# Norm stores and inverse-block loads moved to GpSimd's queue, keys loaded a step later: a chunked RWKV-7 with a SoLU block

## The chip, the cores and the metric

The kernel runs on one core of one Trainium2 chip. The metric is the device time of one execution in microseconds (us). Before the change it was 652.03 us, the median of three runs (650.71, 652.03 and 653.35).

A core has five engines that run at the same time, each with its own list of instructions that it works off in order: TensorE (PE in the profile; PEld are its weight loads), VectorE (DVE), ScalarE (ACT), GpSimd (POOL) and SyncE (SP). They wait for one another through semaphores. SP does no arithmetic here, it only issues DMA transfers; ACT and POOL issue some as well, each from its own list.

## What is computed

Two blocks in a row. The first is a recurrence over 768 tokens, for 4 batches of 8 heads of width 40; its outputs are rows of 320 numbers for 3072 tokens. The second is a feed-forward block with the SoLU activation and a layer norm.

```python
for t in range(S):                                   # S = 768, D = 40, state is D x D per head
    y[:, :, t] = einsum('bhd,bhde->bhe', rt, state)
    Sa = einsum('bhde,bhe->bhd', state, at)
    state_decay = state * wt[:, :, None, :] - einsum('bhd,bhe->bhde', Sa, bt)
    state = state_decay + einsum('bhd,bhe->bhde', vt, kt)
...
h = x @ w_in                                         # x: 3072 x 320, w_in: 320 x 1024
sm = softmax(h)
solu = h * sm
ln = (solu - mean) / sqrt(var + 1e-6) * g_ln
out = ln @ w_out                                     # w_out: 1024 x 320
```

## The kernel before

**Steps.** The recurrence is cut into chunks of 64 tokens. A step i works on one chunk of one pair of batches, with all 8 heads: 12 chunks times 2 pairs make N = 24 steps. Inside a chunk the recurrence becomes matrix products, and one triangular matrix of 64 x 64 for each head must be inverted. That matrix, nt, is made by `norm(i)`: TensorE multiplies a and b (both scaled by the decay), VectorE masks the product (L351), and the result is stored in HBM (`nt_dram`).

**Inverses.** Two steps share one inverse n = i // 2. `invert(n)` first calls `spread(n)`, which loads the 32 x 32 diagonal blocks of both steps' matrices back from HBM in another layout, with four transfers to the tile `blk`. The stored matrices must have landed first. Then VectorE copies and negates half of the blocks (L397) and runs 30 substitution steps of one product (L403) and one subtraction (L405) each. The result goes to HBM (`uu_dram`, L410), and `bring(i)` loads it for each step, into the tiles tu and uh, when it has landed. `flip(i)` transposes part of tu on VectorE (L430). `invert` is a Python generator: `some(n)` takes n substitution steps of it, so that they are spread between other work of VectorE.

**The loop.** The main loop (L774) runs i from -1 to 27 and works on several steps at a time. For step i it finishes the recurrence (`carried`, `driven`, `solved`, `answered`, `read`, `leave`). For i+1 it makes the score matrices (`attend_kv`, `attend_rs`, `scores`, `couple`, `close`). For j = i+5 it prepares the decayed a and b (`front`, which turns a with TensorE, L323, and multiplies it on VectorE, L347) and `norm(j)`, and after every second norm begins an inverse. For steps before i it computes the feed-forward block (`hidden`, `exped`, `weighed`, `spreadof`, `folded`, `output`).

**Order.** The lists of PE, POOL, DVE and SP follow the order of the program's text; only ACT's is arranged by a scheduler. So a transfer leaves SP when all that the program issues on SP before it has been issued and its own waits are met. In a step, SP's list is: `bring(i+1)` (tu and uh), `load_values(i+2)` (v), the keys, the store of `norm(j)`, in every second step the four loads of `spread`, the store of a finished inverse (wherever `some` comes to its end), and four transfers xT of `leave(i)`. POOL's list is: r of `load_values`, b and k scaled by the decay (`scaled(j+1)`, L318, tile kb), six transfers xT of `left(i-1)`, the power rs of the layer norm (L669), two copies v and r (`by_value(i+2)`, L296), and two multiplications of the state st (`leave`, L611).

**Keys.** `load_keys(i, names)` loads w, b, a and k of step i, in two transfers of 80 KB each (L265). w, b and k have three buffers each, a has four.

**Weights.** The feed-forward weights come as 64-bit floats in two words. `land` loads a part of them, and `narrow` and `split` turn the part into 32-bit numbers on VectorE and ScalarE (L182 to L195), between substitution steps, up to i = 3. When a part is done, POOL issues the load of a later one into the freed buffer (L208, L171). `centre_w2` (L218) needs all of w_out.

**Before the loop.** Steps 0 to 3 get their norms, inverse 0 is run and inverse 1 begun. The text from L758 on ends with the last substitution steps of inverse 0, its two `bring` calls, and the keys of steps 5 to 7.

Of the kernel before, what the change touches and what calls it, by code (L numbers as in the profile page):

```python
# [21 lines left out]
GRP = 2  # L22
# [26 lines left out]
def kernel(  # L49
# [18 lines left out]
    nc = tc.nc  # L68
# [67 lines left out]
    def banks(name):  # L136
        return ps1.tile([P, 2, 512], FP32, tag="banks", name=name)
# [12 lines left out]
    def land(n, queue):  # L150
        if n >= len(lands) + NF:
            return
        flat = w2.rearrange("p c n -> p (c n)")
        if n < len(lands):
            kt, x = lands[n]
            if n in (2, 3):
                to = two.tile([P, 512], I64, tag=("e", "lnT")[n - 2], name="bits", bufs=1)
            else:
                y = (0, 1, None, None, 0)[n]
                to = flat[:, 1024 * y:1024 * y + 1024].bitcast(I64)  # L160
            y = 0
            for at in (x,) if kt < 2 else (0, 1):
                for first, last in IN_ROWS[kt]:
                    queue.dma_start(out=to[y:y + last - first], in_=moe_w_in[first:last, 512 * at:512 * at + 512])
                    y += last - first
            landed[n] = [(w_in[:, 2 * kt + x], to, None)]
        else:
            c = n - len(lands)
            tag = ("bits", "e", "lnT", "bits", "e", "lnT", "bits", "lnT")[c]
            to = two.tile([P, DM if tag == "bits" else 512], I64, tag=tag, name="bits", bufs=1)[:, 0:DM]  # L170
            queue.dma_start(out=to, in_=moe_w_out[c * P:(c + 1) * P, :])  # L171
            landed[n] = [(w2[:, c], to, c)]
# [53 lines left out]
    def half(p):  # L226
        return slice(C * p, C * p + C)
# [6 lines left out]
    def in_turn(tile_of, some=units):  # L234

        lots = {}
        for u in some:
            lots.setdefault(tile_of(*u), []).append(u)
        lots = list(lots.values())
        return [lot[n] for n in range(max(map(len, lots))) for lot in lots if n < len(lot)]  # L240

    def mm(o, lhsT, rhs, start=True, stop=True):
        nc.tensor.matmul(o, lhsT=lhsT, rhs=rhs, start=start, stop=stop, skip_group_check=True)  # L243
# [13 lines left out]
    blocks, inverse = {}, {}  # L257
# [4 lines left out]
    def load(x, ap, i, queue=nc.sync):  # L262
        bp, ci = where_(i)
        for p in range(2):
            queue.dma_start(out=x[half(p), :, 0:D],  # L265
                              in_=ap[2 * bp + p, :, ci * C:(ci + 1) * C, :].rearrange("h t d -> t h d"))

    def ok(i):
        return 0 <= i < N


    def load_keys(i, names, queue=nc.sync):
        if not ok(i):
            return
        for n, ap in (("w", w), ("b", b), ("a", a), ("k", k)):
            if n in names:
                x = a_t[i % 4] if n == "a" else two.tile([P, H, D], FP32, tag="raw_" + n, name="raw_" + n,
                                                             bufs=3)
                st[i]["raw_" + n] = x
                load(x, ap, i, queue)  # L280

    def load_values(i):
        if not ok(i):
            return
        d = st[i]
        d["lv"] = two.tile([P, H, W2], FP32, tag="lv", name="lv", bufs=3)
        d["raw_r"] = two.tile([P, H, D], FP32, tag="raw_r", name="raw_r")
        load(d["lv"][:, :, C:], v, i)
        load(d["raw_r"], r, i, nc.gpsimd)
# [37 lines left out]
    def tokens(name, bufs=1):  # L327
        return two.tile([P, 2, 4, C], FP32, tag=name, name=name, bufs=bufs)
# [12 lines left out]
    def front(i):  # L341
        if not ok(i):
            return
        d = st[i]
        t = turned("a", d["raw_a"])
        aT = d["aT"] = tokens("aT", AHEAD)
        nc.vector.tensor_tensor(out=aT[0:W2], in0=t, in1=d["ex"][0:W2, :, :, 0:C], op=ALU.mult)  # L347
        d["bT"] = kept("bT", turned("b", d["kb"][:, H:]))

    def masked(dst, t):  # L350
        nc.vector.tensor_tensor(out=dst, in0=t.rearrange("p b (j c) -> p b j c", j=4),  # L351
                                in1=tri.unsqueeze(1).unsqueeze(1).to_broadcast([P, 2, 4, C]), op=ALU.mult)

    def keyed(t, u):
        p, q, g, h = u
        return t[rows(h), p, 2 * q + g]
# [5 lines left out]
    def norm(i):  # L362
        if not ok(i):
            return
        d = st[i]
        t = banks("pnt")
        for u in in_turn(lambda p, q, g, h: (h, p ^ h)):
            p, q, g, h = u
            j = 2 * q + g
            mm(t[half(p ^ h), h, j * C:j * C + C], keyed(d["bT"], u), keyed(d["aT"], u))  # L370
        nt = d["nt"] = tokens("nt", AHEAD)
        masked(nt, t[:, :, 0:256])
        n, at = divmod(i, GRP)
        if at == 0:
            blocks[n] = dram.tile([2 * GRP * H, C, C], FP32, tag="nt_dram", name="nt_dram")
        nc.sync.dma_start(out=blocks[n].rearrange("(a h x) s c -> a x s h c", a=GRP, x=2)[at].rearrange("x s h c -> (x s) h c"),
                          in_=nt.rearrange("p h j c -> p (h j) c"))


# [1 line left out]
    def spread(n):  # L381
        nb = two.tile([P, Q, Q], FP32, tag="blk", name="blk")
        for y in range(2):
            for e in range(2):
                home = C * y + Q * e
                queue = nc.gpsimd if y and not n else nc.sync
                queue.dma_start(out=nb[home:home + Q], in_=blocks[n][:, Q * e:Q * e + Q, Q * e:Q * e + Q])
        return nb

# [24 lines left out]
    def bring(i):  # L414
        if not ok(i):
            return
        d = st[i]
        d["tu"], d["uh"] = tu_t[i % 2], uh_t[i % 2]
        n, at = divmod(i, GRP)
        src = inverse[n].rearrange("(e a h x) c t -> e a h x c t", e=2, a=GRP, x=2)  # L420
        for x in range(2):
            nc.sync.dma_start(out=d["tu"][C * x:C * x + Q, :, Q:2 * Q], in_=src[0, at, :, x].rearrange("h c t -> c h t"))
        for x in range(2):
            nc.sync.dma_start(out=d["uh"][C * x + Q:C * x + C], in_=src[1, at].rearrange("h x c t -> c (h x) t"))

    def flip(i):
        if not ok(i):
            return
        tu = st[i]["tu"]
        nc.vector.transpose(out=tu[:, :, 0:Q], in_=tu[:, :, Q:2 * Q])  # L430
# [270 lines left out]
    def some(n):  # L701
        while steps and n:
            if next(steps[0], steps) is steps:
                steps.pop(0)
            else:
                n -= 1
# [52 lines left out]
    load_keys(6, "w")  # L759
    land(3, nc.sync)  # L760
    some(14)
    bring(0)
    bring(1)
    load_keys(7, "w")
    load_values(1)
    load_keys(5, "bak")
    for n in (4, len(lands)):
        land(n, nc.sync)
    load_keys(6, "bak")


    shares = {-1: (0, 6, 2, 6), 0: (0, 6, 4, 6), 1: (0, 6, 3, 6), 2: (0, 6, 3, 6), 3: (0, 6, 3, 6)}
# [1 line left out]
    for i in range(-1, N + 3 + LAG):  # L774
        j, m = i + AHEAD, i - LAG
        pieces = shares.get(i, (3, 6, 0, 6))
        some_weights = narrowed.get(i, (0, 0))

        some(pieces[0])
        if i >= 1:  # L780
            bring(i + 1)
        if i >= 0:
            load_values(i + 2)
        carried(i)
        driven(i)
        front(j)
        hidden(m - 2, ((0, 1),))
        load_keys(j + 4, "w")
        load_keys(j + 3, "bak")
        narrow(some_weights[0], pieces[1])  # L790

        solved(i)
        attend_kv(i + 1)
        hidden(m - 2, ((1, 1),))
        attend_rs(i + 1)
        hidden(m - 2, ((2, 0), (2, 1)))
        exped(m - 2)
        decay_turned(j + 1)
        scaled(j + 1)
        left(i - 1)  # L800

        answered(i)
        norm(j)
        if i >= 0:
            flip(i + 1)
        weighed(m - 2)
        spreadof(m - 2)
        decay(j + 2)
        if i == 0:
            turn_g()  # L810
        if i == 3 + LAG:
            centre_w2()
        output(m - 3, 0)
        if ok(j) and j % GRP == GRP - 1:
            begin_inverse(j // GRP)
        some(pieces[2])
        scores(i + 1)
        if i < 0:
            flip(i + 1)
        couple(i + 1)  # L820
        output(m - 3, 1)
        narrow(some_weights[1], pieces[3])

        close(i + 1)
        read(i, True)
        read(i, False)
        by_value(i + 2)
        leave(i)
        folded(m - 2)
        hidden(m - 1, ((0, 0), (1, 0)))  # L830
# [30 lines left out]
```

## Time and profile before

| | |
|---|---|
| median of three runs | 652.03 us |
| the profiled execution's own time | 652.45 us |
| its span, first to last instruction | 650.4 us |
| mean granted TensorE clock | 0.922 |
| TensorE busy (PE) | 562.9 us, 87% |
| TensorE weight loads (PEld) | 400.0 us, 61% |
| VectorE busy | 483.2 us, 74% |
| ScalarE busy | 245.0 us, 38% |
| GpSimd busy | 221.2 us, 34% |
| SP's DMA queue, share of 16 DMA engines | 40.8% |
| POOL's DMA queue, share of 16 DMA engines | 5.9% |

The shares are means over a program with stages that differ. The page's second part cuts the span into 40 slices of 16.3 us and gives the busy tenths of each engine: TensorE stands at 9 from about 195 us to the end, and between 2 and 8 ahead of that; VectorE stands at 7 to 9 from about 33 to 553 us, except for the slices of 65 to 81, 98 to 114 and 179 to 195 us, which show a 6, a 3 and a 6.

A time in the trace is counted from the span's start. `SPq` marks the issue of a transfer by SP. It isn't the transfer: the time shown there is the one in which SP was held by it. On POOL too the row `DMA_DIRECT2D` is the issue. What the data took afterwards is seen where somebody waits for it, or in the chain of waits.

### The profile page before, as it was taken

Reading aid. Unit: us, or ns where it says so; the run is one execution under the profiler, and the core shown is the slowest. Engines: PE = TensorE matmul, PEld = TensorE weight load, DVE = VectorE, ACT = ScalarE, POOL = GpSimd, SP = SyncE. Lnnn points to the kernel's source line nnn. Section 1 sums busy time; section 2 is a strip of 40 time slices with the busy share of each in tenths; the row PEclk is TensorE's granted clock in tenths of the full one; section 3 lists DMA queues with packets and bytes.
Section 4 is the critical chain, followed back from the end, with each engine's and each line's share of the span. In section 5 each row is a group of like instructions: output and inputs, shape, how many; then the busy total and the mean of one; then the engine's idle time right before and its main releaser. Section 6 shows DMA issues by size and latency. Waiting matters only on the chain.

```text
span 650.4 us, 26703 instructions
## 1 busy us (share of the span) xinstructions
PE 562.9 (87%) x11449; PEld 400.0 (61%) x11449; DVE 483.2 (74%) x1285; ACT 245.0 (38%) x497; POOL 221.2 (34%) x384
## 2 busy tenths in 40 slices
PE   5245474887889999999999999999999999999994
PEld 3134462765657676767677667767676767666653
DVE  4678693989967878979888889889897787333431
ACT  3413343355333344244434433443344324332221
POOL 3333222545414234514441453245233422322200
PEclk9666577589799999999999999999999999999998
DMA  8939796667363465466465555554432612310000
GB/s 164 160 70 151 126 164 118 145 128 135 63 106 64 88 113 102 95 112 115 81 114 92 109 96 99 96 100 94 78 70 58 109 38 48 62 38 25 23 20 20
DMA packets 276748, 59.92 MB, mean 92 GB/s; under 512 B 264656, under 2 KB 274488, under 8 KB 276632
## 3 DMA queue, kind: packets, MB, share of 16 engines
q1 hardware_dynamic: 263384, 44.96, 40.8%
q0 software_dynamic: 7856, 8.76, 5.9%
q10 hardware_dynamic: 5392, 4.51, 2.4%
q8 instruction: 90, 1.47, 1.0%
q14 instruction: 26, 0.21, 0.1%
HBM read 40.10 MB, written 13.37 MB: 82 GB/s over the span
## 4 chain that ended last, share of the span: by engine, by line
PE 67%; DVE 15%; DMA 10%; issue 3%; SPq 3%; ACT 1%; POOL 0%; DVEq 0%; POOLq 0%; ACTq 0%
PE h L243 15%; PE po L691 15%; PE pyo L243 7%; DVE prod L403 4%; DVE uu L405 4%; PE px L243 4%; PE pu L243 3%; PE plnT L680 3%; PE ps L243 3%; DMA blk<-nt_dram 3%; DMA nt_dram<-nt 2%; PE pl L243 2%; SPq L265 2%; PE pz L243 2%; PE pk L323 2%
## 5 line engine op out<-in xcount | busy, mean ns | idle before, releaser
L243 PE MATMUL h<-w_in,xT 128*128 128x512 f32 (+1 forms) x288 | 121.0, 612 | 0.0
L403 DVE TENSOR_TENSOR prod<-blk,uu 128x30 f32<-128x30 f32 (+4 forms) x360 | 107.9, 300 | 12.4 <-DMA blk<-nt_dram 2.4
L691 PE MATMUL po<-w,lnT 128*128 128x320 f32 x384 | 113.6, 441 | 3.0 <-DVE w L222 3.0
L405 DVE TENSOR_TENSOR uu<-uu,prod 128x30 f32<-128x30 f32 (+4 forms) x360 | 103.8, 288 | 12.4
L691 PEld LDWEIGHTS po<-w,lnT 128*128 128x128 f32 x384 | 70.4, 190 | 32.6 <-issue 5.8
L669 POOL TENSOR_TENSOR rs<-c,mhalf 128x1 f32<-128x1 f32 x24 | 13.4, 560 | 210.4 <-DVE c L668 210.4
L643 DVE TENSOR_REDUCE nmax<-h 128x1 f32<-128x1024 f32 x24 | 29.4, 1224 | 57.2 <-PE h L243 57.2
L611 POOL TENSOR_TENSOR st<-tot,ex 104x160 f32<-104x160 f32 x44 | 21.3, 501 | 102.4 <-DVE tot L607 102.4
L243 PEld LDWEIGHTS h<-w_in,xT 128*128 128x128 f32 (+1 forms) x288 | 38.8, 189 | 21.4 <-issue 19.3
L623 POOL DMA_DIRECT2D xT<-x x96 | 48.9, 515 | 0.0
L243 PE MATMUL pyo<-lv,kb 64*64 64x104 f32 x768 | 38.3, 272 | 4.9 <-DVE lv L351 2.3
L681 ACT COPY lnT<-plnT 128x512 f32<-128x512 f32 x48 | 26.1, 589 | 43.3 <-PE plnT L680 39.5
L646 ACT ACTIVATE e<-h,nmax 128x1024 f32<-128x1024 f32 x24 | 26.7, 1114 | 28.7 <-DVE nmax L643 27.6
L442 ACT ACTIVATE wy<-py,cst 128x256 f32<-128x256 f32 x24 | 11.4, 474 | 69.3 <-PE py L243 69.3
L243 PE MATMUL pyo<-lu,kb 64*64 64x104 f32 x768 | 37.0, 265 | 0.0
L265 POOL DMA_DIRECT2D raw_r<-in_r_dram x48 | 34.5, 720 | 0.1
L652 DVE TENSOR_TENSOR e<-h,e 128x1024 f32<-128x1024 f32 x24 | 28.8, 1199 | 5.8 <-ACT e L646 5.8
L592 DVE TENSOR_TENSOR x<-pyo,ex 104x256 f32<-104x256 f32 x48 | 18.1, 420 | 18.9 <-PE pyo L243 18.1
L318 POOL TENSOR_TENSOR kb<-raw_b,inv 128x320 f32<-128x320 f32 x24 | 21.4, 891 | 30.5 <-DMA raw_b<-in_b_dram 21.0
L660 DVE BATCH_NORM_STATS2 bs<-e 128x6 f32<-128x512 f32 x48 | 30.9, 685 | 0.8
L695 ACT ACTIVATE osb<-po,rs 128x320 f32<-128x320 f32 x24 | 12.7, 528 | 48.5 <-PE po L691 27.7
L243 PEld LDWEIGHTS pyo<-lv,kb 64*64 64x64 f32 x768 | 23.6, 143 | 10.3 <-issue 7.7
(124 smaller groups left out, 1110.6 us busy)
## 6 DMA issues: line engine op xcount, KB each, us to landing
nt_dram<-nt SPq DMA_DIRECT2D x24, 256.0 KB
blk<-nt_dram SPq DMA_DIRECT2D x46, 128.0 KB
raw_w<-in_w_dram SPq DMA_DIRECT2D x48, 80.0 KB
a<-in_a_dram SPq DMA_DIRECT2D x48, 80.0 KB
raw_r<-in_r_dram POOLq DMA_DIRECT2D x48, 80.0 KB, 3.6
lv<-in_v_dram SPq DMA_DIRECT2D x48, 80.0 KB
out_dram<-osb ACTq DMA_DIRECT2D x24, 160.0 KB
raw_b<-in_b_dram SPq DMA_DIRECT2D x44, 80.0 KB
```

The lines of the kernel that those rows point to most:

```text
L243: nc.tensor.matmul(o, lhsT=lhsT, rhs=rhs, start=start, stop=stop, skip_group_check=True)
L265: queue.dma_start(out=x[half(p), :, 0:D], in_=ap[2 * bp + p, :, ci * C:(ci + 1) * C, :].rearrange("h t d -> t h d"))
L318: nc.gpsimd.tensor_tensor(out=kb[:, j:j + H, 0:D], in0=d["raw_" + n], in1=heads(d["inv"]), op=ALU.mult)
L403: nc.vector.tensor_tensor(out=t, in0=nb[:, j:j + 1, j + 1:Q].to_broadcast([P, n_c, m]), in1=u[:, 0:n_c, j:j + 1].to_broadcast([P, n_c, m]) ...
L405: nc.vector.tensor_tensor(out=u[:, 0:n_c, j + 1:Q], in0=u[:, 0:n_c, j + 1:Q], in1=t, op=ALU.subtract)
L623: nc.gpsimd.dma_start(out=xT[to:to + Q, 2], in_=x[at + P - 3 * D:at + D, 2])
L643: nc.vector.tensor_reduce(out=nmax, in_=d["h"], axis=AX.X, op=ALU.max, negate=True)
L646: nc.scalar.activation(out=e, in_=d["h"], func=AF.Exp, bias=nmax, accum_out=d["esum"])
L652: nc.vector.tensor_tensor(out=d["e"], in0=d["h"], in1=d["e"], op=ALU.mult)
L660: nc.vector.bn_stats(out=bs[:, x], in_=d["e"][:, x * 512:x * 512 + 512])
L681: nc.scalar.copy(out=lnT[:, x * (NF // 2):(x + 1) * (NF // 2)].rearrange("p f t -> p (f t)"), in_=t)
L691: nc.tensor.matmul(d["out"][:, 0:DM], lhsT=d["lnT"][:, f, :], rhs=w2[:, f, :], start=f == 0, stop=f == NF - 1)
```

## The change

`norm` stores its matrix from SP for steps 0 to 3 only, and from POOL for steps 4 to 23. `spread` loads its four blocks from POOL for the inverses 2 to 11; for inverses 0 and 1 nothing is changed (0: two of four from POOL; 1: all from SP).

The keys: in the loop, w is loaded for step j + 3 = i + 8 where it was j + 4, and b, a and k for j + 2 = i + 7 where it was j + 3. Ahead of the loop w(7) and b, a and k of step 6 are no longer loaded. They follow in the loop's first round.

Also ahead of the loop, b and a of step 5 and the values of step 1 (v from SP, r from POOL) are now loaded before `bring(0)` and `bring(1)`, and k of step 5 after them.

```diff
@@ norm @@
-        nc.sync.dma_start(out=blocks[n].rearrange("(a h x) s c -> a x s h c", a=GRP, x=2)[at].rearrange("x s h c -> (x s) h c"),
+        queue = nc.sync if i < 4 else nc.gpsimd
+        queue.dma_start(out=blocks[n].rearrange("(a h x) s c -> a x s h c", a=GRP, x=2)[at].rearrange("x s h c -> (x s) h c"),
                           in_=nt.rearrange("p h j c -> p (h j) c"))
@@ spread @@
-                queue = nc.gpsimd if y and not n else nc.sync
+                queue = nc.gpsimd if n > 1 or y and not n else nc.sync
                 queue.dma_start(out=nb[home:home + Q], in_=blocks[n][:, Q * e:Q * e + Q, Q * e:Q * e + Q])
@@ ahead of the loop @@
     load_keys(6, "w")
     land(3, nc.sync)
     some(14)
+    load_keys(5, "ba")
+    load_values(1)
     bring(0)
     bring(1)
-    load_keys(7, "w")
-    load_values(1)
-    load_keys(5, "bak")
+    load_keys(5, "k")
     for n in (4, len(lands)):
         land(n, nc.sync)
-    load_keys(6, "bak")
@@ in the loop @@
         front(j)
         hidden(m - 2, ((0, 1),))
-        load_keys(j + 4, "w")
-        load_keys(j + 3, "bak")
+        load_keys(j + 3, "w")
+        load_keys(j + 2, "bak")
         narrow(some_weights[0], pieces[1])
```

The lists of PE and DVE hold the same instructions in the same order as before. One line more in `norm` shifts the line numbers after it by one in the changed kernel (L376 becomes L377, and so on).

## The prediction

> **What bounds the kernel now.** First the busy time of each engine by stretches of the span (columns: stretch, its length, then PE, PEld, DVE, ACT and POOL busy with counts, granted clock, DMA share, GB/s):
>
> ```profile
> 68.00:77.00 9.00, 3.43 (x98) 3.19 (x99) 5.68 (x17) 3.48 (x7) 0.86 (x1) 0.50 0.67 108
> 77.00:99.00 22.00, 17.65 (x456) 14.92 (x455) 20.23 (x55) 10.24 (x23) 8.31 (x11) 0.74 0.93 168
> 99.00:110.00 11.00, 5.42 (x82) 4.01 (x82) 1.29 (x7) 6.21 (x13) 2.74 (x5) 0.79 0.83 140
> 110.00:182.00 72.00, 55.22 (x1268) 42.89 (x1268) 66.78 (x188) 30.82 (x63) 34.32 (x56) 0.77 0.60 115
> 220.00:487.00 267.00, 263.94 (x5785) 187.72 (x5783) 229.68 (x601) 109.61 (x224) 103.23 (x180) 1.00 0.52 97
> ```
>
> Two regimes. From 220 us to the end of the inverses TensorE is busy 264 of 267 us: nothing that only reorders DMA issues can win there. From 77 to 182 us VectorE is the full engine (20.2 of 22, 66.8 of 72), with a hole from 99 to 110 us in which it works 1.3 us and nobody else is full. A smaller hole lies before it, in 68 to 77. So the second view is what VectorE waited for there, in order of time:
>
> ```profile
> 77.70 0.69 DVE L347 TENSOR_TENSOR aT<-pa,ex 104x512 f32<-104x512 f32 x1 [3.61 <-PE pa L323]
> ...
> 98.09 0.68 DVE L347 TENSOR_TENSOR aT<-pa,ex 104x512 f32<-104x512 f32 x1
> 98.69 0.32 DVE L182 TENSOR_SCALAR scale<-bits 128x320 int32<-128x320 int32 x1
> 98.92 0.32 DVE L183 TENSOR_SCALAR w<-bits 128x320 int32<-128x320 int32 x1
> 99.40 0.48 DVE L395 MEMSET uu<- 64x512 f32 x1 [0.16 <-issue]
> 99.97 0.07 DVE L396 MEMSET uu<- 64x16 f32 x1
> 108.19 0.42 DVE L397 TENSOR_SCALAR uu<-blk 64x512 f32<-64x512 f32 x1 [8.16 <-DMA blk<-nt_dram]
> 108.69 0.07 DVE L398 MEMSET uu<- 64x16 f32 x1
> 110.00 0.19 DVE L403 TENSOR_TENSOR prod<-blk,uu 128x30 f32<-128x30 f32 x1 [1.24 <-DMA blk<-nt_dram]
> ```
>
> In brackets stand the idle time and what ended it: 3.61 us for TensorE's turning of a(5), then 8.16 and 1.24 us for blk(2), the blocks of the third inverse. TensorE's own line says where the first comes from:
>
> ```profile
> 76.60 1.07 PE L323 MATMUL pa<-cst,a 128*104 128x128 f32 x4 [4.78 <-DMA a<-in_a_dram]
> ```
>
> It waited for a(5) itself. The third view is SP's list of issues, which tells why a(5) and blk(2) are late:
>
> ```profile
> 68.88 1.32 SPq L265 DMA_DIRECT2D raw_w<-in_w_dram  x2
> 70.25 1.47 SPq L265 DMA_DIRECT2D lv<-in_v_dram  x2
> 71.81 1.27 SPq L265 DMA_DIRECT2D raw_b<-in_b_dram  x2
> 73.19 1.27 SPq L265 DMA_DIRECT2D a<-in_a_dram  x2
> ...
> 92.45 0.57 SPq L376 DMA_DIRECT2D nt_dram<-nt  x1
> ...
> 100.34 0.57 SPq L376 DMA_DIRECT2D nt_dram<-nt  x1
> 103.66 3.16 SPq L387 DMA_DIRECT2D blk<-nt_dram  x4
> ```
>
> SP issues without a pause from 68.9 to 101 us. nt(4) was masked by VectorE at 62.6 us and its store goes out at 92.45; nt(5) was masked at 87.0 and goes out at 100.34. These are 30 and 13 us of queueing behind key loads, not of transfer: the chain of waits gives 3.30 us for the store's landing and 3.67 for the last block's. The data of a(5), wanted at 71.8 when px ends, is issued at 73.19, behind bring(0), bring(1), a w, and values.
>
> [...] here sequencer time is what is short (13 to 30 us lost), while the DMA share at 99 to 110 us is 0.83. [...] the trace has medians of 2.3 us to landing for POOL's xT pieces, 3.6 for raw_r, 4.5 for the two POOL blk loads. [...] POOL's blk issues show 0.81 and 0.98 us each. [...] L397 takes 0.42 us alone (108.19) and 2.48 us at 247.93, beside raw_r's issue from 247.78.
>
> **The change, part by part.**
>
> *(1) b(5), a(5) and lv(1) ahead of bring(0).* SP is idle from 59.4 (second uu_dram issue) until uu_dram(0) has landed at 64.6. Six issues of 0.64 us fill 59.4 to 63.3. So a(5) lands by about 66 to 67 instead of 76.6. Price: the four tiles' loads of bring(0) queue behind 480 KB on the same DMA queue. I take half of this to be through by 64.6, since the DMA share was 0.54 in 62 to 64 and 0.10 in 64 to 66, and charge 0.7 us on tu(0), flip(0) and what follows (bounds 0 and 2). Then pa can start at 71.8 + 0.7 = 72.5, and VectorE, which is busy with the weight split until 74.10 + 0.7 = 74.8, runs aT(5) at once: 77.70 - 74.8 = **2.9 us** won, of the 3.61 that it idled. Next late: nothing; ACT's lw(7) now stands behind ex in its list, not ahead of bT, so w(7), issued about 72, holds nobody. k(5) goes from 74.63 to about 69.5 and w, b, k of later steps are still issued a step (some 20 us) ahead of their use.
>
> *(2) Keys one step later.* As many loads as before, later. It takes k(6), w(8), b/a/k(7), w(9) and b/a/k(8), 18 issues of 0.64 us, out of 77 to 101 us at the place where they stood ahead of the stores. With (3) SP reaches uu_dram(1) by about 85 us, before VectorE has it ready (94.9 - 2.9 = 92), so the issue at 106.91 becomes about 92, and tu(2), issued at 111.94 before, about 98. Cost: nothing; b(7), first used by POOL at 115.25, is issued by 82.
>
> *(3) nt(4..23) and blk(2..11) on POOL.* Twenty stores and forty block loads leave SP. On POOL I charge 0.9 us for each, from the two blk rows (a store has as many rows of 64 numbers as a block load has of 32). nt(4) goes out behind kb(5), about 73.5, instead of 92.45. nt(5): masked at 87.0 - 2.9 = 84.1; ahead of it on POOL are a weight load freed by the split (86.06 - 2.9 = 83.2, 0.6 us) and kb(6) (two of 0.87), so it starts at 85.5, and lands by 89 with raw_r's 3.6. The blocks follow, 89 to 92.6, the last landing 3.5 to 4.5 us after its start: 95.2 to 96.2. VectorE wants them at L397 at 99.97 + 0.07 - 2.9 = 97.1. So both waits, 8.16 + 1.24 = 9.4 us, go, with one or two us in hand. New on the path: raw_r(3) is issued behind tot, at about 96.2 to 97.6, beside L397; I charge 0.5 us (bounds 0 and 2.06, the 2.48 less 0.42). Net 8.9.
>
> What is late next: lu(1), which ran at 114.26 after these steps. VectorE would be there at 114.26 - 2.9 - 8.9 = 102.5; TensorE's pl(1) ended at 105.77 and moves by 2.9 only, to 102.9. So lu(1) runs at 102.9: **11.4 us** earlier. From there to 182 VectorE is full, so its list shifts as a block; then pmean and TensorE take over, with all inputs shifted too.
>
> blk(3) must keep up: nt(7) masked 137.1 - 11.4 = 125.7, but POOL is at xT(1) until 140.6 - 11.4 = 129.2; store to 130.1, landed 132.8, blocks to 136.4, landed 140; L403 wanted them at 152.26 - 11.4 = 140.9. It fits, closely. Behind blk on POOL are a weight load, v, r and st, by 0.5 us late at most.
>
> In the full stretch a pair of steps adds 2 x 0.9 + 4 x 0.9 = 5.4 us to POOL, which works 103 of 267 us. The order there is nt, rs, blk, v, r, st. With the step at 228 to 262: nt masked 237.1, landed 240.7, blk to 244.7, v and r to 245.6, against tot at 246.9, which st waits for in any case, and pv at 253.3. Hidden by 1.3 us for st and 7.7 for TensorE. I charge 0.
>
> Sum: 2.9 + 8.5 = 11.4. Against its own execution: span 650.4 - 11.4 = 639.0, time 652.45 - 11.4 = 641.05. That execution lies 0.42 above the median 652.03; on the median it is **640.6 us**.
>
> **Rivals.**
> A (forecast): both holes close, 9 to 14 us, 638 to 643. The upper end is no price on tu and a pl(1) that also gains; the lower has 2 us on tu or L397 blocked in full.
> B: the first hole closes, blk(2) stays late on POOL. For it: POOL issues in order[...]. Two or so us per block instead of 0.9, and 6 instead of 3.6 for the store, put the last landing at 102 to 104: 5 to 7 us of 9.4 are back, leaving 5 to 6: 645 to 648. Against: the two blk issues at 24.2 took 1.8 us together, under a DMA share near 1.
> C: the gain is swallowed after 110, by VectorE blocked by POOL's 5.4 us per pair. VectorE's products in the inverse kept 0.25 to 0.27 us beside xT issues at 117 to 119, which speaks against; it would give 649 to 652.
> D (slower): blk's wait on POOL. In each of eight steady pairs POOL stands at blk until the store has landed; v for pv has 7.7 us of slack. If landing plus issues take 7.7 + x us more than I have, TensorE waits x per pair. To undo 11.4 us and lose 4, x = 15.4/8 = 1.9, so a landing of over 13 us; time 656. The longest landing of any raw_r is 5.4 us, so it is unlikely.
>
> That the instructions don't move is excluded: TensorE's and VectorE's lists are unchanged, SP's and POOL's hold the moved rows.
>
> **How the numbers follow.** A 0.65, B 0.17, C 0.08, D 0.10. One measurement of this kernel tells 0.5%, 3.3 us, from no change. Faster: A, and B nearly whole (0.17): 0.82; same: most of C: 0.08; slower: D: 0.10. Range 637 to 648: A and B hold 0.82, the low end one us under A's.
>
> **What would show it.** VectorE without the bracketed waits at aT(5), L397 and the first L403; POOL's nt(5) issue near 85 and blk near 89; lu(1) near 103; steps from 220 on unchanged at 22.2 us. Wrong if L397 of the third inverse still waits for blk, if flip(0) moves beyond 69.5, or if TensorE shows new waits for v or st.

## The result, and the profile after

The changed kernel takes 642.57 us (median of four runs, 642.36 to 643.25) against 652.69 us for the kernel before on the same chip: a ratio of 0.985 (95% interval 0.9822 to 0.9877), 10.1 us less. A second set of runs later gave 643.34 against 653.33 us, the same ratio (0.9816 to 0.9885). The profiled execution took 642.36 us with a span of 640.3.

First VectorE, in order of time, in the changed kernel, with the steps at which it had waited before. The columns are start, duration, engine, line, operation, and in brackets the idle time before it and what ended it:

```profile
74.97 0.68 DVE L347 TENSOR_TENSOR aT<-pa,ex 104x512 f32<-104x512 f32 x1
...
97.25 0.42 DVE L398 TENSOR_SCALAR uu<-blk 64x512 f32<-64x512 f32 x1
97.78 0.19 DVE L404 TENSOR_TENSOR prod<-blk,uu 128x30 f32<-128x30 f32 x1
...
103.08 0.69 DVE L351 TENSOR_TENSOR lu<-pl,cst 128x512 f32<-128x512 f32 x1 [0.94 <-PE pl L243]
```

The brackets of 3.61, 8.16 and 1.24 us are gone, and what limits next is what stands in the last line: lu(1) waits 0.94 us for TensorE's pl(1). It runs at 103.08 instead of 114.26, 11.2 us earlier.

The busy times of the changed kernel in three stretches (stretch, length, then PE, PEld, DVE, ACT and POOL busy with counts, granted clock, DMA share, GB/s):

```profile
74.00:96.00 22.00, 18.14 (x444) 15.38 (x443) 20.63 (x55) 10.70 (x24) 13.44 (x19) 0.66 0.99 188
96.00:103.00 7.00, 4.83 (x68) 3.99 (x68) 5.38 (x21) 5.08 (x10) 2.64 (x4) 0.76 0.50 92
220.00:487.00 267.00, 264.32 (x5847) 188.64 (x5846) 231.65 (x609) 110.03 (x225) 133.44 (x220) 1.00 0.50 99
```

The stretch in which nobody was full has no counterpart: VectorE works 5.4 of the 7 us from 96 to 103. In the last line POOL went from 103 to 133 of 267 us while TensorE stayed at 264: the added issues are hidden there.

GpSimd's own list shows the stores and the blocks at their new place:

```profile
85.47 0.95 POOL L377 DMA_DIRECT2D nt_dram<-nt  x1
89.79 3.13 POOL L388 DMA_DIRECT2D blk<-nt_dram  x4 [3.38 <-DMA nt_dram<-nt]
...
96.69 1.38 POOL L265 DMA_DIRECT2D raw_r<-in_r_dram  x2
```

nt(5) is stored at 85.47 instead of 100.34, and four block issues take 3.13 us after a wait of 3.38 us for the store. SP's list of the changed kernel has got short:

```profile
58.05 4.43 SPq L265 DMA_DIRECT2D raw_b<-in_b_dram  x2
62.60 1.28 SPq L265 DMA_DIRECT2D a<-in_a_dram  x2
63.92 1.31 SPq L265 DMA_DIRECT2D lv<-in_v_dram  x2
65.33 1.06 SPq L423 DMA_DIRECT2D tu<-uu_dram  x2
...
92.21 2.34 SPq L411 DMA_DIRECT2D uu_dram<-uu  x2
```

a(5) goes out at 62.6 instead of 73.2, uu_dram(1) at 92.2 instead of 106.9. The price of the first is in the first four lines: the loads occupy SP until 65.2, so tu(0) is issued at 65.33, 8.7 us after uu_dram(0); before, it was 6.5 us (58.08 to 64.60).

So the head of the program gains 11.2 to 12.3 us, yet the whole 10.1. VectorE's list of the changed kernel against that of the kernel before, instruction by instruction, shows where the rest went (worked out from the two traces' start times; the second row of numbers is the changed kernel less the one before):

```
start before  shift in us
 78.98   -2.7
110.00  -12.2
115.82  -11.2
164.64  -12.3
185.22  -10.7
224.80   -9.3
299.74   -9.5
498.65   -9.9
617.22   -9.9
```

Between lu(1) and 165 us 1.1 us more is won: a product that took 1.27 us at 115.82 takes 0.22 us now, at 104.64. Between 165 and 225 us 3.0 us are lost, and 0.6 comes back later. The experiments first take the gain apart, then this loss.

### The profile page after: what moved, and what is told of

It reads as the page before. It is cut to its first block, busy times and chain, and to the rows that moved or that the text cites. A ratio compares the mean times of both kernels' runs of the same rounds, so it can differ in the third digit from the quotient of the medians.

```text
span 640.3 us, 26725 instructions
## 1 busy us (share of the span) xinstructions
PE 565.3 (88%) x11449; PEld 400.6 (63%) x11449; DVE 483.0 (75%) x1285; ACT 245.1 (38%) x497; POOL 269.1 (42%) x444
## 2 busy tenths in 40 slices
DMA packets 217868, 59.92 MB, mean 94 GB/s; under 512 B 203216, under 2 KB 213048, under 8 KB 217752
## 3 DMA queue, kind: packets, MB, share of 16 engines
q1 hardware_dynamic: 200984, 34.47, 31.8%
q0 software_dynamic: 11376, 19.25, 12.5%
## 4 chain that ended last, share of the span: by engine, by line
PE 70%; DVE 15%; DMA 7%; issue 3%; ACT 3%; SPq 1%; ACTq 0%; DVEq 0%; POOL 0%; POOLq 0%
PE po L692 16%; PE h L243 14%; PE pyo L243 7%; DVE prod L404 4%; PE pu L243 3%; PE px L243 3%; DVE uu L406 3%; PE ps L243 3%; DMA xT<-x 3%; PE plnT L681 2%; PE pl L243 2%; PE pz L243 2%; PE pei L323 2%; PE pk L323 2%; PE pr L323 2%
## 5 line engine op out<-in xcount | busy, mean ns | idle before, releaser
L404 DVE TENSOR_TENSOR prod<-blk,uu 128x30 f32<-128x30 f32 (+4 forms) x360 | 120.2, 334 | 16.4 <-DMA blk<-nt_dram 6.3
L692 PE MATMUL po<-w,lnT 128*128 128x320 f32 x384 | 115.2, 445 | 3.0 <-DVE w L222 3.0
L406 DVE TENSOR_TENSOR uu<-uu,prod 128x30 f32<-128x30 f32 (+4 forms) x360 | 105.7, 294 | 12.4
L377 POOL DMA_DIRECT2D nt_dram<-nt x20 | 18.6, 929 | 89.1 <-DVE nt L351 76.3
L612 POOL TENSOR_TENSOR st<-tot,ex 104x160 f32<-104x160 f32 x44 | 22.2, 521 | 78.9 <-DVE tot L608 78.2
L388 POOL DMA_DIRECT2D blk<-nt_dram x42 | 33.3, 798 | 18.0 <-DMA nt_dram<-nt 17.7
L318 POOL TENSOR_TENSOR kb<-raw_k,inv 128x320 f32<-128x320 f32 x24 | 21.6, 901 | 20.5 <-DMA raw_k<-in_k_dram 20.5
```

The source lines that it names most:

```text
L404: nc.vector.tensor_tensor(out=t, in0=nb[:, j:j + 1, j + 1:Q].to_broadcast([P, n_c, m]), in1=u[:, 0:n_c, j:j + 1].to_broadcast([P, n_c, m]) ...
L406: nc.vector.tensor_tensor(out=u[:, 0:n_c, j + 1:Q], in0=u[:, 0:n_c, j + 1:Q], in1=t, op=ALU.subtract)
L692: nc.tensor.matmul(d["out"][:, 0:DM], lhsT=d["lnT"][:, f, :], rhs=w2[:, f, :], start=f == 0, stop=f == NF - 1)
```

## Experiments on the three parts

All runs of this section were compared with the kernel before on one chip, except keys_pool, which was measured later beside its own runs of the kernel before.

**order_only.** The order part alone.

```diff
     some(14)
+    load_keys(5, "ba")
+    load_values(1)
     bring(0)
     bring(1)
     load_keys(7, "w")
-    load_values(1)
-    load_keys(5, "bak")
+    load_keys(5, "k")
```

> Only a(5), b(5) and lv(1) go ahead of the first inverted blocks; keys 7 and 6 and all stores and block loads stay where they were, on SP. Theory (the list of SP is one line; whatever stands ahead of nt(5) in it makes blk(2) late): aT(5) starts without a bracketed wait at about 75, 2.9 us earlier, and SP's list after it runs some 3 to 4 us earlier too, so the second hole (9.4 us) is not smaller in VectorE's time by more than about 1 us: 3 to 4 us below before, about 649. Rival (the first hole is only moved into the second): 0 to -1 us.

Measured: 651.61 us, ratio 0.9967 (0.9947 to 0.9987), 2.2 us less. VectorE in order_only:

```profile
73.38 0.68 DVE L347 TENSOR_TENSOR aT<-pa,ex 104x512 f32<-104x512 f32 x1
...
103.65 0.42 DVE L397 TENSOR_SCALAR uu<-blk 64x512 f32<-64x512 f32 x1 [7.86 <-DMA blk<-nt_dram]
...
105.41 0.19 DVE L403 TENSOR_TENSOR prod<-blk,uu 128x30 f32<-128x30 f32 x1 [1.19 <-DMA blk<-nt_dram]
```

The first wait is gone, the second is as long as before (7.86 us against 8.16), since SP's list behind it moved along: the second store goes out at 96.10 instead of 100.34. lu(1) comes at 109.67, 4.6 us earlier, of which 1.0 stood already at 63 us, before VectorE waits for anything that a moved issue brings. In the head the rival (hole one moves into hole two) falls. In the whole time the run lies between the two expectations (2.2 us, interval 0.8 to 3.5).

**keys_only.** The keys part alone: in the loop `j + 3` and `j + 2` for `j + 4` and `j + 3`, and ahead of it

```diff
     bring(1)
-    load_keys(7, "w")
     load_values(1)
...
         land(n, nc.sync)
-    load_keys(6, "bak")
```

> Only the keys of steps 6 and 7 leave the stretch from 77 to 101 us (18 issues of 0.64 us); stores and block loads stay on SP, the first hole stays. Theory that the keys on SP's list are the cause of the late blk(2): nt(5) is issued near 91 instead of 100.3, blk(2) near 94 to 97, landed near 101, so that the waits at the first uu and prod of the solve (8.2 and 1.2 us) shrink to about 1 to 2 us together: 7 to 8 us below before, about 645. Rival (GpSimd's queue is needed for it, as I took in the prediction): at most 3 us below before.

Measured: 648.64 us, 0.9929 (0.9905 to 0.9953), 4.6 us less in the whole, and 7.8 at lu(1) (106.48). VectorE in keys_only:

```profile
74.47 0.69 DVE L347 TENSOR_TENSOR aT<-pa,ex 104x512 f32<-104x512 f32 x1 [2.56 <-PE pa L323]
...
99.59 0.42 DVE L397 TENSOR_SCALAR uu<-blk 64x512 f32<-64x512 f32 x1 [2.37 <-DMA blk<-nt_dram]
...
102.21 0.19 DVE L403 TENSOR_TENSOR prod<-blk,uu 128x30 f32<-128x30 f32 x1 [2.05 <-DMA blk<-nt_dram]
```

9.4 us of waiting for blk(2) have become 4.4. SP stores nt(5) at 92.61 and starts on the blocks at 95.77; both are near the times that the theory had, but the waits shrink by less (4.4 us are left, not 1 to 2). The wait at aT(5) is shorter too, since w(7) no longer stands ahead of a(5) on SP. In the whole the run fell between the two expectations; the part lost after 110 us is the subject of the next section.

**pool_only.** The GpSimd part alone (the first two pieces of the diff above).

> Only the stores from step 4 on and the blocks from the third pair on go through GpSimd's queue; order and keys as before. Theory: aT(5) keeps its wait (starts near 77.7), nt(5) goes out near 89.5, blk(2) lands near 100, and the waits of 9.4 us at the solve's first uu and prod are gone but for 1 us; the first lu after it is then held by pl(1) near 105.8 as the keys still lie on SP: about 8.5 us below before, near 644. Rival (GpSimd's issues cost as much in its own work as they take from SP): 4 us or less below before.

Measured: 646.65 us, 0.9916 (0.9882 to 0.9949), 5.5 us less; lu(1) at 105.62, 8.6 us earlier. aT(5) waits 3.67 us as before, blk(2) costs one wait of 0.49 us at the first product. The rival falls for the head; the whole again falls short of the head by some 3 us.

**order_keys.** The changed kernel without its GpSimd part: stores and blocks stay on SP.

> The changed kernel without its GpSimd part: order and keys as changed, stores and block loads all on SP. Theory (three substitutes for one hole): nt(5) on SP near 91 or earlier, blk(2) landed near 100, the first lu of the solve near 105 instead of 103: 8 to 9 us below before, 1 to 2 us short of the changed kernel. Rival (the parts add up, GpSimd's queue carries most of it): only 3 to 4 us below before. If it is as fast as the changed kernel or faster, GpSimd's part brings nothing that the keys do not.

Measured: 646.23 us, 0.9906 (0.9879 to 0.9933), 6.1 us less. VectorE in order_keys:

```profile
74.89 0.68 DVE L347 TENSOR_TENSOR aT<-pa,ex 104x512 f32<-104x512 f32 x1
...
99.28 0.42 DVE L397 TENSOR_SCALAR uu<-blk 64x512 f32<-64x512 f32 x1 [2.36 <-DMA blk<-nt_dram]
...
101.90 0.19 DVE L403 TENSOR_TENSOR prod<-blk,uu 128x30 f32<-128x30 f32 x1 [2.05 <-DMA blk<-nt_dram]
```

The order part removed the wait at aT(5), 2.56 us in keys_only, and yet lu(1) moved by 0.3 us only (106.17 against 106.48). aT(5) itself did not come earlier: 74.89 against 74.47. The keys_only execution was 0.8 us further ahead at 63 us, where neither edit can act yet, and flip(0) ran there at 65.24 instead of 67.68; part of this is the price of the order part, since SP issued tu(0) 8.4 us after uu_dram(0) and not 6.9. Then the two lists of SP show a second thing, keys_only first:

```profile
92.61 0.96 SPq L376 DMA_DIRECT2D nt_dram<-nt  x1
95.77 2.19 SPq L387 DMA_DIRECT2D blk<-nt_dram  x4
```

```profile
90.51 0.57 SPq L376 DMA_DIRECT2D nt_dram<-nt  x1
95.10 2.85 SPq L387 DMA_DIRECT2D blk<-nt_dram  x4
```

With the order part SP stored nt(5) 2.1 us earlier, but the chain of waits gives 4.58 us for that store's landing and 3.15 in keys_only, so the blocks went out only 0.7 us earlier. Why this store landed late no run tells.

In the whole 6.1 us are less than the 8 to 9 expected and more than the rival's 3 to 4. Beside the changed kernel (0.9822 to 0.9877) the intervals are just apart: GpSimd's part brings some 4 us that order and keys do not bring.

**keys_pool.** The changed kernel without its order part.

> The changed kernel without its order part: keys one step later and GpSimd's queue as changed, the inverted blocks ahead of step 5's a and b as before. Theory (the order part brings its 2.9 us only where nothing later sets the end of the head): the wait of 2.6 us at aT(5) comes back, nothing else does; blk(2) lands near 98 and VectorE does not wait for it; the second lu after it at about 105.7 instead of 103.1, so 2.6 us slower than the changed kernel, about 7.5 us below before. With order_keys against keys_only (0.3 us between them at that lu) this gives the order part's two worths. Rival (the order part is worth as little here as there): within 0.5 us of the changed kernel.

Measured: 646.29 us, 0.9879 (0.9844 to 0.9914), 7.9 us less. The wait at aT(5) is back (3.06 us). lu(1) comes at 104.62: 1.5 us later than in the changed kernel, not 2.6. VectorE now waits 1.39 us for blk(2)'s last block, which I had excluded, and in exchange not for pl(1), where the changed kernel stood for 0.94. At lu(1) the rival (within 0.5 us) is less likely than the theory; one execution each doesn't exclude it, as the spread below shows. In whole times, by the ratios, 1.9 us lie between the two, and their intervals overlap.

The six side by side, by the start of lu(1), where the head ends. Each start is that of one profiled execution, and so is that of the kernel before. All six were ahead of it before VectorE waits for anything that a moved issue brings; the third column of numbers is that lead, at the instruction that ran at 63.38 us before:

```
parts              lu(1)    gain there   lead at 63   left    gain in the whole
order              109.67      4.6          1.0        3.6          2.2
keys               106.48      7.8          1.6        6.2          4.6
GpSimd             105.62      8.6          0.8        7.9          5.5
order, keys        106.17      8.1          0.7        7.4          6.1
keys, GpSimd       104.62      9.6          0.5        9.1          7.9
all three          103.08     11.2          0.7       10.5         10.1
```

Five profiled executions whose kernels are the same up to here (the changed kernel twice, after_keep, after_keep5 and after_split below) have lu(1) between 102.03 and 103.16, so a difference of about 1 us in this table is not told from chance.

What stands clear of that: keys and GpSimd are two cures for one delay, that of blk(2) behind SP's list. Alone they leave a gain of 6.2 and 7.9 us, 14.1 in sum, and together 9.1. The three single parts add up to 17.7 us, the joint gain is 10.5. What the order part is worth is less sure: 3.6 us alone, and a little over 1 us beside the keys, with GpSimd or without. In whole times the overlap of the parts isn't shown: 2.2, 4.6 and 5.5 us make 12.3, and with intervals of 1.3 to 2.2 us to either side this isn't told from 10.1.

## Experiments on the loss after 165 us

In every profile above 1.4 to 3.5 us of the head's gain were lost behind lu(1). What differs there, for the most part, is the granted TensorE clock. It changes on a grid of 3.41 us: in the clock records of both kernels every stretch at one clock, but for the last, lasts a whole multiple of 3.413 us. The first po after the centred weights is such a place; first the kernel before, then the changed one, in the two windows around it (columns as above, the clock is third from the end):

```profile
187.30:190.71 3.41, 1.79 (x7) 0.95 (x5) 2.55 (x6) 0.00 (x0) 1.36 (x3) 1.00 0.64 115
190.71:194.12 3.41, 2.02 (x8) 1.44 (x8) 1.25 (x1) 0.00 (x0) 0.00 (x0) 1.00 0.83 88
```

```profile
177.80:181.21 3.41, 0.60 (x3) 0.09 (x1) 2.77 (x1) 0.00 (x0) 3.12 (x5) 1.00 0.25 72
181.21:184.62 3.41, 3.22 (x6) 2.19 (x7) 0.05 (x1) 0.00 (x0) 1.39 (x3) 0.50 0.32 84
```

Both kernels have the same wait of 3.0 us for w. Before, it happened to be split over two windows, TensorE was busy 1.79 and 2.02 us in them, and the clock stayed. In the changed kernel it fell into one, 0.60 us busy, and the next ran at half the clock. The matmuls show it, the kernel before first, then the changed one:

```profile
192.10 2.39 PE L691 MATMUL po<-w,lnT 128*128 128x320 f32 x8 [3.01 <-DVE w L222]
```

```profile
181.40 3.98 PE L692 MATMUL po<-w,lnT 128*128 128x320 f32 x8 [3.00 <-DVE w L222]
```

The eight take 3.98 us instead of 2.39. The thirteen profiles of this study (before, the changed kernel twice, ten variants) have, between 160 and 230 us, 13 windows at full clock in which TensorE was busy 12 to 45% and which were followed by a window at half clock, and 17 with 46 to 71% which were not (my own count over the records; windows above 75% are left out). None of the 13 was idle.

The price of a halved window can be read off VectorE's list in two stretches, told here by the times of the kernel before.

From 164.6 to 185.2 us TensorE waits for aT, while VectorE is late. Nine profiles waited 2.05 to 2.58 us there, had a halved window behind it and lost 1.35 to 1.68 us. keys_only waited 0.98 us and lost nothing, although a window was halved at 167.17, ahead of that wait. The two variants with raw_r on SP (below) waited 1.44 us and not at all, had no halved window and won 0.9.

From 189 to 225 us TensorE waits for w, as shown above. With no halved window there the loss is nothing (0.0 to 0.2 us won, six profiles, after_keep5 below among them; after_keep, whose fill held po up, lost 2.0), with one it is 1.4 (the changed kernel) and 1.5 us (pool_only).

The kernel before has no halved window that begins later than 167. Not all that was lost behind lu(1) is this: the 1.4 us of keys_only, 1.1 of the 2.3 of keys_pool and 0.8 of the 3.5 of pool_only went before 165. keys_pool waited there for the blocks of the fourth inverse, 0.70 us at 141.74 and 1.64 at 144.11.

**after_again.** The changed kernel, unaltered.

> The changed kernel itself, a second look. Theory that the clock windows lie by chance on a grid of 3.41 us and that each halved one past 165 us costs about 1.6 us: 9 to 11 us below before, with one to two halved windows between 165 and 190 us and a span of 639 to 641.5; every step of the head (the a of step 5 near 75, the blocks issued near 90, the second lu near 103) within 0.7 us of the first look. Rival (the loss after 160 us belongs to the program, not to the clock): the same loss of 2 to 3 us with full clock there.

Measured: 9.8 us below before by the ratio 0.985; its profiled execution has a span of 643.0, more than the 641.5 allowed. lu(1) is at 103.16, the blocks at 90.92 (89.79 in the first execution: 1.1 us apart, more than the 0.7 allowed). Three halved windows begin after 165 us (one at 168.5, two from 182.1 on) where one or two were expected. From 165 to 225 us it lost 4.4 us against the kernel before with three halved windows, and the first execution 3.0 with two: 1.5 us a window in both. The rival (the same loss at full clock) isn't seen. From lu(1) to 225 us the two executions of one kernel differ by 2.6 us.

**after_keep** and **after_keep5.** Ten, and then five, matmuls whose results are overwritten fill TensorE's wait for w.

```diff
             d["out"] = bank("po")
+            for c in range(10 if i == 0 else 0):
+                nc.tensor.matmul(d["out"][:, 0:DM], lhsT=c_("mean"), rhs=w_in[:, 0, 0:DM], start=True, stop=True)
```

> The changed kernel with ten matmuls of 128x320 more ahead of the first po, into po's own bank, which the real ones overwrite: they fill TensorE's wait of 3.0 us for w at about 178.4 to 181.4. Theory (that wait leaves the window idle, and the clock is halved in the next one): ten times 0.28 is 2.8 us, so po starts no later than 181.6, the window from 181 on has clock 1.0, the eight po take 2.4 us instead of 3.98, and the kernel is 1.6 us faster than the changed one (near 641.0). Rival (idle TensorE has nothing to do with it, or the clock follows an earlier stretch): the window stays halved and the time the same or up to 1 us longer.

> The changed kernel with five matmuls of 128x320 more ahead of the first po. Ten took 5.37 us in the run before (0.54 each, two passes of a weight load and a product), not the 2.8 I had worked out, and held po up by 2.2 us; five take 2.7 and end as w comes. Theory (idle TensorE halves the clock of the next window): po starts within 0.2 us of w, at clock 1.0, eight records in 2.4 us instead of 3.98, and the kernel is 1.6 us faster than the changed one, or by as much as halved windows past 178 us cost in it. Rival: a halved window there in spite of them, no gain.

Measured: ten: 644.05 us, 0.9867 (0.9839 to 0.9894). They were mis-sized, as the second text says, and delayed po from 182.6, when w had come, to 184.8; the next window kept full clock, and the eight took 2.32 us. Five: 642.52 us, 0.9836 (0.9804 to 0.9867). With five, the windows around po and TensorE's list there:

```profile
179.55:182.96 3.41, 3.33 (x13) 2.02 (x11) 2.74 (x1) 0.00 (x0) 3.12 (x5) 1.00 0.25 61
182.96:186.37 3.41, 3.27 (x68) 2.36 (x72) 0.08 (x1) 0.00 (x0) 1.43 (x3) 1.00 0.34 95
```

```profile
180.02 2.85 PE L692 MATMUL po<-w_in,cst 128*128 128x320 f32 x10
183.10 2.42 PE L694 MATMUL po<-w,lnT 128*128 128x320 f32 x8 [0.22 <-DVE w L222]
```

The window is busy, the next has full clock, po takes 2.42 us. From 189 to 225 us VectorE's list, which had lost 1.4 us in the changed kernel (2.8 in its second execution), gains 0.2. So idle TensorE is what halved this window, and it cost 1.6 us: shown in this place, by one profile of each kernel. In the median of whole runs it isn't to be told from nothing (0.9836 against 0.985, intervals overlapping): this profile has another halved window at 169.3, with 38% busy ahead of it, which the matmuls don't touch.

**after_split.** The wait itself is shortened.

```diff
-        nc.vector.tensor_tensor(out=w2, in0=w2, in1=t[:, 0:DM].unsqueeze(1).to_broadcast([P, NF, DM]),
-                                op=ALU.subtract)
+        for c in range(0, NF, 2):
+            nc.vector.tensor_tensor(out=w2[:, c:c + 2], in0=w2[:, c:c + 2], in1=t[:, 0:DM].unsqueeze(1).to_broadcast([P, 2, DM]), op=ALU.subtract)
```

> The changed kernel with the one subtraction of 128x2560 (w less its mean, 2.82 us on VectorE) cut into four of 128x640. po's first matmuls need the first piece alone: TensorE waits about 0.8 to 1.0 us instead of 3.0, po starts near 179.3 instead of 181.4 and is done near 182 to 183; VectorE waits for psi's ps anyhow (5.29 us at L351). Theory: 2 us faster than the changed kernel from the wait, and 1.6 more if the clock stays full since TensorE is less idle: 2 to 3.6 us, near 639 to 640.5. Rival (the four pieces cost more, or what follows waits for something else): 0 to 0.5 us.

Measured: 640.28 us, 0.9809 (0.9781 to 0.9837), 3.1 us less than the changed kernel in the same set of runs (0.9816 to 0.9885, so the intervals overlap a little). TensorE in after_split:

```profile
179.89 2.39 PE L692 MATMUL po<-w,lnT 128*128 128x320 f32 x8 [1.00 <-DVE w L223]
```

The wait is 1.00 us instead of 3.00, the four pieces take VectorE 3.02 us instead of 2.82, and the clock stays full (71% busy in that window). The profile bears the theory out: from 189 to 225 us VectorE's list wins 2.2 us where the changed kernel lost 1.4, 2 us of it from the wait and 1.6 from the clock.

**after_rsp.** raw_r from step 2 on through SP.

```diff
-        load(d["raw_r"], r, i, nc.gpsimd)
+        load(d["raw_r"], r, i, nc.gpsimd if i < 2 else nc.sync)
```

> The changed kernel with raw_r's loads from step 2 on taken from GpSimd's queue back to SP's. Theory (raw_r's issues lie beside VectorE's products and hold some of them up): the product of 128x126 at about 161.7 takes 0.3 to 0.9 us instead of 2.70, the same in every odd step, and L398 goes from 0.89 to 0.42; aT behind the first of these is 1.5 to 2.4 us earlier, so TensorE's wait at pv (2.43 us) goes, which is worth up to 2 us with the halved window after it; in the steady steps nothing changes, since TensorE bounds them: 0 to 3 us faster than the changed kernel. Rival (the hold comes from the additions and kb on GpSimd, not from the issue): the 2.70 stays and the time is the same. Rival (SP's list gets late again by 1.3 us a step): slower by 0 to 1 us.

What had put me on it are two lines of VectorE in the changed kernel, a product that takes 0.28 us elsewhere, with GpSimd's list below them:

```profile
161.70 2.70 DVE L404 TENSOR_TENSOR prod<-blk,uu 128x126 f32<-128x126 f32 x1
164.44 0.83 DVE L406 TENSOR_TENSOR uu<-uu,prod 128x126 f32<-128x126 f32 x1
```

```profile
160.87 1.11 POOL L612 TENSOR_TENSOR st<-tot,ex 104x160 f32<-104x160 f32 x2 [8.24 <-DVE tot L608]
161.93 1.42 POOL L265 DMA_DIRECT2D raw_r<-in_r_dram  x2
163.37 0.88 POOL L318 TENSOR_TENSOR kb<-raw_b,inv 128x320 f32<-128x320 f32 x1
```

Measured: 642.16 us, 0.9824 (0.979 to 0.9859), 1.2 us less than the changed kernel, with overlapping intervals, so not told apart from it. My theory that raw_r's issue is what holds VectorE falls: the product takes 0.29 us, but the operation next to it takes its place, in after_rsp, with no issue on GpSimd beside it until its last 0.2 us:

```profile
159.54 2.49 DVE L406 TENSOR_TENSOR uu<-uu,prod 128x120 f32<-128x120 f32 x1
```

It spans GpSimd's st and both kb (159.17 to 161.89). It isn't new either: in the kernel before, four operations at the same point took 1.06, 0.83, 1.18 and 0.82 us instead of 0.28 each, 2.8 us in all, as much as the two lines above (3.0). raw_r's issue can have stretched the block: the hold costs 2.2 us here instead of 3.0, and TensorE's wait for aT, of 2.07 to 2.43 us in the five profiles of kernels with raw_r on GpSimd and all three parts, is 1.44 here and gone in split_rsp. Neither of these two has a halved window after 159 us. The profiled execution of after_rsp is the shortest of all (span 635.8); in the median the gain isn't shown.

**split_rsp.** Both of the last two edits.

> The changed kernel with both: the subtraction of w's mean in four pieces, and raw_r's loads from step 2 on through SP. If the gains lie apart (1.7 to 3.7 us in VectorE's time for the pieces, 2 to 4 us for raw_r, of which the clock is a part in both): 3 to 5 us faster than the changed kernel, 638 to 640. If both only recover the same halved window: 2 us, no faster than the pieces alone.

Measured: 639.04 us, 0.9783 (0.9752 to 0.9813): 14.2 us below the kernel before and some 4 us below the changed one by the ratios, the fastest of the study. Its interval lies just clear of the changed kernel's (0.9816 to 0.9885, and 0.9822 to 0.9877 in the first set), not of after_split's.

## Why the prediction was right, and where it was off

- *What bounds the kernel*: right. SP's list, not any transfer, made a(5) and blk(2) late. Unloading it in different ways closes the first hole (3.61 us to none with the order part), or half and more of the second (9.4 us to 4.4 with the keys, to 0.5 with GpSimd).
- *Step 1, the order*: 2.9 us predicted, 2.73 measured at aT(5) (77.70 to 74.97). This agreement is in part luck: 0.7 us stood already at 63 us, so 2.0 are left. The price was set too low. flip(0) came 0.4 us later (67.43 to 67.84) in an execution that was 0.7 us ahead, so it cost 1.1 us where 0.7 was charged. By the issue of tu(0) it was more: SP issued it 8.2 to 9.0 us after uu_dram(0) in the nine profiles with the order part, and 5.9 to 7.1 in the four without, some 2 us, the upper bound that the prediction gave. SP did not reach the end of the six issues by 63.3 but by 65.2, because the pair of raw_b was held for 4.43 us instead of 1.3 (3.9 to 4.8 in all nine). What held it no run here tells.
- *Step 2, the keys*: the times were right (uu_dram(1) near 92: 92.21; tu(2) near 98: 98.31). I gave this step no gain of its own, since step 3 already took both waits. Alone it is worth some 6 to 8 us in the head: most of the same gain could have been booked to either.
- *Step 3, GpSimd*: nt(5) at 85.5 predicted, 85.47; blocks 89 to 92.6, 89.79 to 92.92; issue price 0.9 us for each, 0.93 for a store and 0.78 for a block; the last landing before VectorE came to it, as no wait shows. The margin is thin: in keys_pool and pool_only VectorE waited 1.39 and 0.49 us for the last block. raw_r beside L397, charged at 0.5 us, cost nothing: L398 took 0.42 us with raw_r's issue around it. So standing beside raw_r's issue is not enough to make it 2.48 us, as the prediction read the copy at 247.93. That one runs on into kb on GpSimd; but in the changed kernel the same copy, begun 0.15 us into the same issue, took 0.42 us in each of the last eight inverses. What decides between the two no run tells. In after_rsp the held subtraction (2.49 us, 0.28 elsewhere) stood beside elementwise operations of GpSimd, st and both kb (159.17 to 161.89), three of them in a row, and an issue lies beside its last 0.2 us alone. So an issue isn't needed for such a hold; that these operations are its cause I read from what ran beside it, and no run tests it.
- *What is late next*: pl(1) at 102.9 predicted as the limit; lu(1) ran at 103.08 after waiting 0.94 us for pl. 11.2 us against 11.4. That the two are so close is luck as well: the lead of 0.7 us is in the 11.2, and four other executions with the same head put lu(1) between 102.03 and 103.16.
- *From there on*: "VectorE is full, so its list shifts as a block" held until 165 us (12.3 us). Behind it stands a term that I did not have: the clock. I took the durations of the profiled execution as they were, and a shift of the whole list as harmless. But the windows of the clock, 3.41 us each, do not shift along, and the two gaps of 2.4 and 3.0 us at 164 and 178 us fell into one window each (TensorE busy 29 and 18% of it), and the next window ran at half clock both times. The term was left at zero and measured 3.0 us between 165 and 225. The rest of the way made up for more than half of it: 11.2 us at lu(1), 1.1 more by 165, 3.0 lost, 0.6 back later make 9.9 us on VectorE's list and 10.1 in the span; hence 10.1 us in place of 11.4, and 642.6 in place of 640.6.
- *The rivals*: B (blocks late on GpSimd) is not seen at blk(2): four block issues took 3.13 us, beside a DMA share of 0.70 from 88 to 93 us. (The prediction took the DMA share beside the two issues at 24.2 as near 1; from 24 to 26 us it was 0.50.) Later blocks did come late: VectorE waited 2.07 us for them at 285.62 and 2.02 at 506.36, where the kernel before had one such wait after 110 us, of 1.18. Nothing was lost by it, since the shift is 9.9 us at 498.65 and at 617.22. C (gain swallowed by VectorE held by GpSimd) is not seen either: TensorE's steps from 220 us on are as long as before (the first half of po starts at 227.45 and 249.63 us, 22.2 apart; before at 236.76 and 258.99). D would need waits for v or st; none is there.

## What to carry to other kernels

When one queue of issues makes two things late, ask of each remedy what it is worth beside the others: by the start of lu(1), keys and GpSimd each seemed to bring most of the gain, and together they brought far less than their sum. Before comparing two profiles by a start time, look at a point that the change can't have reached yet: here the executions already differed by up to 2.1 us there. Cost a gap on TensorE by its length and by what it may do to the next clock window, and treat the second as a matter of chance, worth here some 1.5 us (1.35 to 1.68) for each gap of two to three us; of the two remedies tried, shortening the gap (the four pieces) gave the lower time, filling it gave none that could be told from nothing.

## What the runs showed of the hardware that was not expected

- The granted clock was halved after windows of 3.41 us in which TensorE had been busy up to 45% (13 cases), and kept after 46 to 71% (17 cases), from 160 us on. From 20 to 160 us every window with less than 49% was followed by half clock as well, but so were some with 50 to 70%, so the share that the records give isn't the whole rule.
- GpSimd's issues took nearly the same time each: 0.92 to 0.95 us for a store, 0.78 for a block (784 ns median of the 24 from 225 to 487 us, 784 to 832), where SP took 0.30 to 2.19 us for blocks of the same size.
- The same bytes (59.92 MB) went in 217868 packets instead of 276748: with the stores and blocks on GpSimd's queue, the two queues' shares of the DMA engines went from 40.8 and 5.9% to 31.8 and 12.5%, 2.4 points less in sum.
